# First batch's attention: gates in two passes on VectorE, products and decode kept in PSUM, q's factors from TensorE

## The chip, the cores and the metric

The kernel runs on one NeuronCore of a Trainium2 chip. The metric is the device time of one execution in microseconds (us), the median of several. The engines are TensorE (PE, with its weight loads PEld), VectorE (DVE), ScalarE (ACT) and GpSimd (POOL); SyncE (SP) issues the DMAs. Each runs its own instructions in order, and waits for the others by semaphores.

## The reference, cut to what matters

There are 4 batches of 8 heads, 768 positions and 40 features a head. An mLSTM attention is followed by a mixer of two two-layer perceptrons.

```python
for t in range(S):
    m_new = maximum(f[t] + m, i[t])
    f_stab, i_stab = exp(f[t] + m - m_new), exp(i[t] - m_new)
    C = f_stab * C + i_stab * outer(v[t], k[t]);  n = f_stab * n + i_stab * k[t]
    y[t] = sigmoid(o[t]) * (C @ q[t]) / maximum(abs(n @ q[t]), 1)
x = y.transpose(0, 2, 1, 3).reshape(4, 768, 320)
u = x + (maximum(x.T @ w_tok1, 0) @ w_tok2).T
out = u + maximum(u @ w_ch1, 0) @ w_ch2
```

## The kernel before, in words

The sequence is cut into 6 chunks of 128 positions; a unit is one batch and one chunk, u0 to u5 those of the first batch. Within a unit the attention is a masked product of scores and values, and a state `C` (40 x 41 a head) carries over what lies before it.

The gates give two rows for each head: `phi`, the running sum of the log decays within a chunk, and `b`. They come from a scan for the running maximum, two additions, a second scan and two subtractions (`gate_phi`, `gate_b`, lines 99 to 122), 36 partitions wide; `split` makes a bf16 remainder of them on 9 partitions. They are made in three passes, chunk 0, chunk 1 and chunks 2 to 5, the last one partly on GpSimd.

For the first batch TensorE spreads phi and b over a 128 x 128 tile for each head (`spread_split`), and ScalarE takes the exponential (`prep_exp`) into `dd`. `st_s` makes the scores `ps_sc` and `st_p` multiplies them into `dd` on VectorE. `prep_q3` scales q by `pq`, the exponential of phi on q's layout: for u1 and u2 from TensorE (`spread_q`), for u3 to u5 from a DMA that reads phi back from DRAM (`phi_d`, line 223). `prep_kw` scales k by `wcol`. `st_state` multiplies q with the old state into `po`, and kw with v into `pu`; VectorE masks `pu` (`bm_t`, a constant that a DMA brings) and adds the decayed state. `st_pv` adds the products with v to `po`. ScalarE copies `po` to `ht` (line 393), GpSimd multiplies it by the sigmoid of o (line 401), VectorE makes the divisor `den` (407 to 411) and the result `x` (421), and x is written as two fp32r parts, `xh` on ScalarE and `xl` on GpSimd.

The mixer's weights arrive as 30 pieces of 384 columns of 8 bytes each and are decoded beside the attention: two ScalarE operations a piece (559, 560), two VectorE operations (573, 577), the high part on ScalarE (588) and the low part on GpSimd (594). `dec_ops` is a generator of two pieces whose steps are placed by hand among other work.

The order on every engine is written out by hand in the main body (from line 696): an opening for u0 to u2 with 4 decoded pieces in it, a loop over c = 1 to 3 with two pieces a pass, and a closing part with 4 more. Then `a_part` multiplies w_tok1 with x of the six units (36 matmuls of 320 columns), and `a_end` writes its result `rh` (line 617). From there the mixer of the first batch runs in slots of one `gemm1` and one `gemm2`, with two more weight pieces a slot until all 30 are done, and later batches' attention is laid between the slots of the batch ahead. `warm` issues matmuls on zeros.

Of the kernel before, what the change touches and what calls it, by code (L numbers as in the profile page):

```python
# [18 lines left out]
L = 128  # L19
# [15 lines left out]
def kernel(ctx: ExitStack, tc: tile.TileContext, gates, qk, q3, kv, og,  # L35
                            wt1, wt2, wc1, wc2, ident, bmask, sel, out):
# [15 lines left out]
    def load_sig(b, i):  # L52
# [6 lines left out]
    floor_b = wp.tile([128, 1], F32, name="floor_b")  # L59
    nc.gpsimd.memset(floor_b, 2.0 ** -14 - 0.5)  # L60
# [36 lines left out]
    chunks = [x.rearrange("p (c t) -> p c t", t=L) for x in (b_t, d_t, phi)]  # L97

    def gate_phi(c0, c1, between=None):
        lo, hi = c0 * L, c1 * L  # L100
        sl = slice(lo, hi)
# [3 lines left out]
        if between:  # L105
            between()
        if lo == 0:
            v.tensor_tensor(d_t[:, 1:hi], f_t[:, 1:hi], m_t[:, 0:hi - 1], ALU.add)
            v.tensor_copy(d_t[:, 0:1], m_t[:, 0:1])
        else:  # L110
            v.tensor_tensor(d_t[:, sl], f_t[:, sl], m_t[:, lo - 1:hi - 1], ALU.add)
        nc.gpsimd.tensor_tensor(b_t[:, sl], i_t[:, sl], m_t[:, sl], ALU.subtract)
        v.tensor_tensor(d_t[:, sl], d_t[:, sl], m_t[:, sl], ALU.subtract)
        v.tensor_tensor_scan(phi[:, sl], rst2[:, sl], d_t[:, sl], 0.0, op0=ALU.mult, op1=ALU.add)

    def gate_b(c0, c1, eng=nc.vector):
# [200 lines left out]
    def st_state(u):  # L317
# [14 lines left out]
        if c < NC - 1:  # L332
# [36 lines left out]
    def st_pv(u, copy=True):  # L369
# [5 lines left out]
        po = t["po"] if c else ps_m.tile([128, H, E1], F32, tag="m", name="po")  # L375
# [8 lines left out]
        if u == (0, NC - 1):  # L384
            t["ht"] = po
        elif copy:
# [9 lines left out]
    def st_hs(u):  # L396
# [4 lines left out]
        (nc.vector if u == (0, NC - 1) else nc.gpsimd).tensor_tensor(sg, sg, ht[:, :, 0:D], ALU.mult)  # L401
# [12 lines left out]

    def x_ops(u):
# [126 lines left out]
    his, lows, wx = [], [], []  # L542
# [12 lines left out]
    def dec_abs(n):  # L555
        while nxt[1] < min(n, len(pieces)):
            raw = staged[nxt[1]]
            f = wq.tile([128, WP], F32, tag="wf", name="wf", bufs=4)
# [3 lines left out]
            ready[nxt[1]] = f  # L562
            nxt[1] += 1

    def dec_ops(more, m=2):
# [4 lines left out]
        ps = [(staged.pop(m), ready.pop(m)) + pieces[m] for m in range(n, min(n + m, len(pieces)))]  # L570
# [136 lines left out]
    load_phi(u0)
    load_phi(u1)
    load_phi(u2)
    nc.vector.tensor_copy(id_b, id_t)  # L710
    nc.gpsimd.tensor_tensor(id3, id_b[:, 0:H], id_b[:, 64:64 + H], ALU.add)
    nc.gpsimd.tensor_tensor(id3, id3, id_b[:, 96:96 + H], ALU.add)
    T[u0]["phi"] = r = [spread_late(ps_h, "h") for _ in range(2)]
    gate_phi(0, 1)
# [12 lines left out]
    gate_phi(1, 2, lambda: cols_out(t, 0, 1))
    gate_b(1, 2)
    split(1, 2)
    gate_d(1, 2)  # L730
# [31 lines left out]
    step(dg, 9)
    dec_abs(4)
    st_pv(u0, copy=False)
    load_kv(u2)
    dec_load(6)
    st_ht(u0)
    dec_hi()
    spread_split(u2)
    t = cols(2, NC)  # L770
    dg = dec_ops(0)
    step(dg, 3)
    cols_out(t, 2, NC)
    step(dg, 1)
    prep_exp(u2, 0)
    prep_exp(u2, 1)
    st_state(u1)
    step(dg, 9)
    spread_q(u2)
    load_pq(u2, q32)  # L780
    st_hs(u0)
    dec_low()
    prep_q3(u2)
    dec_hi()
    dec_abs(6)
    prep_kw(u2)
    load_phi(u3)
    load_qk(u3, 0)
# [251 lines left out]
```

## Time and profile before

| | us |
|---|---|
| median of 3 runs | 465.51 (465.49 to 466.0) |
| profiled execution | 467.8 |
| its span, first to last instruction | 466.0 |
| PE busy | 441.1 (95%) |
| DVE, ACT, POOL busy | 311.5, 187.0, 139.5 |
| mean granted clock of PE | 0.96 |

[...] Times in rows count from the start of the span. PE's busy time is modelled for matmuls that overlap, so a busy PE need not be one at its peak.

### The profile page before, as it was taken

What the parts mean: (1) busy time and instruction counts of PE and PEld (TensorE: products, weight loads), DVE (VectorE), ACT (ScalarE), POOL (GpSimd) and SP (SyncE); (2) the same over time, 40 slices, a digit from 0 to 9 for tenths busy, and PEclk for the clock granted to TensorE, in tenths of its full rate; (3) what the DMA queues carried; (4) which work ended last, traced back from release to release, by engine and by line L of the source; (5) the groups of instructions that cost most, each with busy time, mean ns of one, the idle gap of its engine ahead of it and who ended that gap; (6) DMA issues with size and microseconds to landing.
All of it is one profiled execution on the core that took longest, in us unless ns stands there. A gap on an engine that the chain in (4) does not pass through costs nothing.

```text
span 466.0 us, 9347 instructions
## 1 busy us (share of the span) xinstructions
PE 441.1 (95%) x3691; PEld 420.7 (90%) x3691; DVE 311.5 (67%) x665; ACT 187.0 (40%) x434; POOL 139.5 (30%) x165
## 2 busy tenths in 40 slices
PE   7669797899999998999999999999999999999997
PEld 3558686799999998999999999999999999999996
DVE  4987787877356747778888578879888555323222
ACT  4526537698634446334233335523431411212111
POOL 4466665146304435031343123034134210000000
PEclk9857878999999998999999999999999999999999
DMA  8745864576036783232274421323422000000000
GB/s 255 221 145 155 219 184 156 195 250 167 2 121 209 210 263 125 73 104 75 67 208 146 145 72 71 93 104 92 123 91 71 30 1 30 1 0 30 1 30 28
DMA packets 25032, 53.16 MB, mean 114 GB/s; under 512 B 2577, under 2 KB 13781, under 8 KB 24989
## 3 DMA queue, kind: packets, MB, share of 16 engines
q1 hardware_dynamic: 24797, 52.39, 36.8%
q8 instruction: 29, 0.48, 0.4%
q10 hardware_dynamic: 192, 0.18, 0.1%
q14 instruction: 14, 0.11, 0.1%
HBM read 48.51 MB, written 4.04 MB: 113 GB/s over the span
## 4 chain that ended last, share of the span: by engine, by line
PE 74%; DMA 10%; DVE 7%; ACT 5%; issue 2%; SPq 1%; POOL 0%; DVEq 0%; ACTq 0%
PE ps_h L600 26%; PE acc L600 25%; DMA pq<-phi_d 5%; PE ps_sc L268 4%; PE ps_a L600 4%; PE ps_b L600 4%; DVE wf L573 3%; PE po L358 3%; PE po L380 3%; DVE wf L577 2%; PE pu L337 2%; PE po L363 2%; DMA wst<-in_wt_dram 2%; DMA wst<-in_wc_dram 1%; DMA sig<-in_og_dram 1%
## 5 line engine op out<-in xcount | busy, mean ns | idle before, releaser
L600 PE MATMUL ps_h<-uT,c1h 128*128 128x256 f32 x720 | 140.3, 282 | 1.7 <-ACT uT L650 0.9
L600 PEld LDWEIGHTS ps_h<-uT,c1h 128*128 128x128 f32 x720 | 115.5, 188 | 2.8 <-ACT uT L650 1.2
L667 ACT ACTIVATE gh<-ps_h 128x512 fp32r<-128x512 f32 x72 | 42.9, 596 | 179.3 <-PE ps_h L600 179.3
L600 PE MATMUL ps_h<-uT,c1l 128*128 128x256 f32 x432 | 111.3, 280 | 0.0
L668 DVE SCALAR_TENSOR_TENSOR gl<-ps_h,gh 128x512 fp32r<-128x512 f32 x72 | 49.5, 688 | 85.8 <-ACT gh L667 85.5
L600 PE MATMUL acc<-c2h,gh 128*128 128x320 f32 x288 | 90.9, 323 | 0.0
L600 PE MATMUL acc<-c2l,gh 128*128 128x320 f32 x288 | 87.2, 310 | 0.0
L600 PEld LDWEIGHTS ps_h<-uT,c1l 128*128 128x128 f32 x432 | 81.3, 188 | 0.0
L600 PE MATMUL acc<-c2h,gl 128*128 128x320 f32 x288 | 66.4, 312 | 0.6 <-DVE gl L668 0.6
L600 PEld LDWEIGHTS acc<-c2h,gh 128*128 128x128 f32 x288 | 54.4, 189 | 1.3
L401 POOL TENSOR_TENSOR sig<-sig,ht 128x320 f32<-128x320 f32 x23 | 20.3, 883 | 114.8 <-DVE ht L366 103.4
L600 PEld LDWEIGHTS acc<-c2l,gh 128*128 128x128 f32 x288 | 54.6, 189 | 0.0
L600 PEld LDWEIGHTS acc<-c2h,gl 128*128 128x128 f32 x288 | 48.6, 190 | 1.3 <-DVE gl L668 1.3
L249 ACT ACTIVATE dd<-dd,bcol 128x128 f32<-128x128 f32 x144 | 45.8, 391 | 7.9 <-POOL dd L239 7.8
L433 POOL TENSOR_TENSOR xl<-x,xh 128x320 fp32r<-128x320 f32 x23 | 21.0, 914 | 48.9 <-DVE xh L429 46.8
L278 DVE TENSOR_TENSOR dd<-ps_sc,dd 128x512 f32<-128x512 f32 x48 | 31.1, 680 | 5.1 <-PE ps_sc L268 5.1
L573 DVE SCALAR_TENSOR_TENSOR wf<-wf,wst 128x384 int32<-128x384 int32 x30 | 25.5, 866 | 10.4 <-POOL q3t L235 4.9
L268 PE MATMUL ps_sc<-raw 40*128 40x128 f32 x384 | 30.5, 297 | 0.0
L380 PE MATMUL po<-kvt,dd 128*128 128x41 f32 (+1 forms) x192 | 26.1, 297 | 3.6 <-issue 1.8
L380 PEld LDWEIGHTS po<-kvt,dd 128*128 128x128 f32 x192 | 25.3, 210 | 4.4 <-issue 1.9
L268 PEld LDWEIGHTS ps_sc<-raw 40*128 40x128 f32 x384 | 25.6, 198 | 4.0 <-issue 2.4
L239 POOL TENSOR_SCALAR_AFFINE_SELECT dd<-dd 128x1024 f32<-128x1024 f32 x18 | 21.9, 1216 | 3.6 <-DMA dd<-phi_d 2.2
(129 smaller groups left out, 776.7 us busy)
## 6 DMA issues: line engine op xcount, KB each, us to landing
dd<-phi_d SPq DMA_DIRECT2D x18, 512.0 KB
wst<-in_wc_dram SPq DMA_DIRECT2D x22, 384.0 KB
kvt<-in_kv_dram SPq DMA_DIRECT2D x24, 324.0 KB
raw<-in_qk_dram SPq DMA_DIRECT2D x48, 160.0 KB
sig<-in_og_dram SPq DMA_DIRECT2D x8, 480.0 KB
out_dram<-x SPq DMA_DIRECT2D x24, 160.0 KB
q3t<-in_q_dram SPq DMA_DIRECT2D x20, 180.0 KB
pq<-phi_d SPq DMA_DIRECT2D x18, 180.0 KB
```

The lines of the kernel that those rows point to most:

```text
L239: nc.gpsimd.affine_select(dd, dd, pattern=[[0, H], [1, L]], compare_op=ALU.is_ge, fill=-1e30, base=0, channel_multiplier=-1)
L249: nc.scalar.activation(dd[:, h, :], dd[:, h, :], AF.Exp, bias=bcol[:, c, HP * b + h:HP * b + h + 1])
L268: nc.tensor.matmul(t["s"][hf][:, h, :], r[:, 1, h, :], r[:, 0, h, :], start=True, stop=True)
L278: nc.vector.tensor_tensor(dd, t["s"][hf], dd, ALU.mult)
L358: nc.tensor.matmul(po[:, h - h0, 0:j1 - j0], p[i][:, ROW[h], :], w[:, h, j0:j1], start=h == h0 and i + j0 == 0, stop=c == 0 and h == h1 - ...
L380: nc.tensor.matmul(o, t["dd"][:, ROW[h], :], x, start=c == 0 and h == 0, stop=h == H - 1)
L401: (nc.vector if u == (0, NC - 1) else nc.gpsimd).tensor_tensor(sg, sg, ht[:, :, 0:D], ALU.mult)
L433: (nc.vector if u == (0, 4) else nc.gpsimd).tensor_tensor(xl, x, f32(xh), ALU.subtract)
L573: v.scalar_tensor_tensor(fi, fi, 3, raw[:, :, 0], op0=ALU.logical_shift_left, op1=ALU.bitwise_or)
L600: nc.tensor.matmul(ps, a, m, start=(first and i == 0), stop=(last and i == n - 1))
L667: nc.scalar.activation(gh, ps, AF.Relu)
L668: nc.vector.scalar_tensor_tensor(gl, ps, 0.0, f32(gh), op0=ALU.max, op1=ALU.subtract)
```

## The change

The unit loop and all later batches keep their formulas. The first batch's part is rewritten. Constants that came by DMA (`sel`) or from VectorE (`id_b`) are made on GpSimd, and `z` is cleared by VectorE. The gates go in two passes, chunk 0 and chunks 1 to 5, all on VectorE.

```diff
-    def gate_phi(c0, c1, between=None):
+    def gates_of(c0, c1):
         v.tensor_tensor_scan(m_t[:, sl], f_t[:, sl], i_t[:, sl], ...)
-        nc.gpsimd.tensor_tensor(b_t[:, sl], i_t[:, sl], m_t[:, sl], ALU.subtract)
+        v.tensor_tensor(d_t[:, sd], f_t[:, sd], m_t[:, sm], ALU.add)
+        v.tensor_tensor(d_t[:, sd], d_t[:, sd], m_t[:, sd], ALU.subtract)
+        v.tensor_tensor_scan(phi[:, sl], rst2[:, sl], d_t[:, sl], 0.0, ...)
+        v.tensor_tensor(b_t[:, sl], i_t[:, sl], m_t[:, sl], ALU.subtract)
+        v.tensor_tensor(b_t[:, sl], b_t[:, sl], phi[:, sl], ALU.subtract)
 ...
     def spread_q(u):
-        ps = ps_m.tile([120, 3, L], F32, tag="m", name="ps_q")
+        ps = ps_h.tile([120, 3, L], F32, tag="h", name="ps_q")
-            nc.tensor.matmul(ps[:, g, :], sel_t[:, g * 120:(g + 1) * 120], phi[:, c * L:(c + 1) * L], ...)
+            nc.tensor.matmul(ps[:, g, :], sel3[:, g], top(z[:, 0, c * L:(c + 1) * L]), ...)
 ...
     def load_pq(u, q3t):
-            if u not in (u1, u2):
+            if b:
                 nc.sync.dma_start(out=pq.rearrange(...), in_=phi_d[...])
 ...
     def st_state(u):
+            cm = cn if c == 0 else puf
-                nc.vector.tensor_tensor(cn[0:p, a:z], puf[0:p, a:z], bm_t[0:p, a:z], ALU.mult)
+                nc.vector.tensor_tensor(cm[0:p, a:z], puf[0:p, a:z], bm_t[0:p, a:z], ALU.mult)
-                    nc.vector.scalar_tensor_tensor(cn[sl], Cst[b][sl], t["decay"][...], cn[sl], ...)
+                    nc.vector.scalar_tensor_tensor(cn[sl], Cst[b][sl], t["decay"][...], cm[sl], ...)
 ...
+    def x0_ops(u):
+        po, n = T[u]["po"], T[u]["bank"][:, 400:400 + H]
+        v.tensor_tensor(po[:, :, 0:D], po[:, :, 0:D], sig[...], ALU.mult)
+        yield
+        v.tensor_scalar(den, po[:, :, D], 1.0, None, op0=ALU.max)
+        v.scalar_tensor_tensor(n, po[:, :, D], -1.0, den, op0=ALU.mult, op1=ALU.max)
+        v.reciprocal(den, n)
+        yield
+        v.tensor_tensor(x.rearrange(...), po[:, :, 0:D], den.unsqueeze(2).to_broadcast(...), ALU.mult)
+        nc.scalar.activation(xh, x, AF.Copy)
+        (v if c == NC - 1 else nc.gpsimd).tensor_tensor(xl, x, f32(xh), ALU.subtract)
 ...
     def dec_abs(n):
-            f = wq.tile([128, WP], F32, tag="wf", name="wf", bufs=4)
+            if early[0]:
+                f = ps_acc.tile([128, WP], F32, tag="acc", name="pf")
+            else:
+                f = wq.tile([128, WP], F32, tag="wf", name="wf", bufs=4)
 ...
     def dec_ops(more, m=2):
-            v.scalar_tensor_tensor(fi, raw[:, :, 1], -0x80000000, fi, ...)
+            v.scalar_tensor_tensor(w.bitcast(I32), raw[:, :, 1], -0x80000000, f.bitcast(I32), ...)
 ...
+    for c in range(1, NC):
+        dg = dec_ops(0)
+        st_s(n1, mid=dg)                  # c < NC - 1, else step(dg, 9)
+        spread_q(n1); prep_q3(n1); prep_kw(n1)
+        dec_load(nxt[2] + 4)
+        st_state(u)
+        step(dg, 9)
+        st_pv(u)
+        load_kv(n2); load_q3(n2)
+        x0 = x0_ops(u); step(x0, 2)
+        spread_split(n2)
+        dec_hi(); prep_exp(n2, 0); prep_exp(n2, 1); dec_low()
+        dec_abs(nxt[2] + 2)
+        step(x0, 9)
+    early[0] = False
```

The loop now runs over c = 1 to 5 (the conditions on c are cut above); 10 pieces are decoded in it, none before it, and 2 after it, so that 12 stand decoded at `rh` where 14 did. `warm(10)` is added ahead of u1's spread. The SP queue brings, ahead of the loop: f, raw and kv of u0, sigmoid input, raw of u1, sigmoid input, two weight pieces, q of u1, the mask `bm_t`, kv of u1, two weight pieces, then u2's.

VectorE from the second gate pass on. Before, it works on chunks 2 to 5 after u0's products (dd), and the first mask (Cn) comes last:

```order
L278 TENSOR_TENSOR dd<-ps_sc,dd 128x512 x2
L133 COPY bcol<-gt 128x36
L103 SCALAR_TENSOR_TENSOR m_t<-f_t,m_t,i_t 36x512
L111 TENSOR_TENSOR d_t<-f_t,m_t 36x512
L113 TENSOR_TENSOR d_t<-d_t,m_t 36x512
L114 SCALAR_TENSOR_TENSOR z<-rst,d_t 36x512
L118 TENSOR_TENSOR z<-z 36x512
```

The same place now, chunks 1 to 5:

```order
L115 SCALAR_TENSOR_TENSOR m_t<-f_t,m_t,i_t 36x640
L118 TENSOR_TENSOR d_t<-f_t,m_t 36x640
L290 TENSOR_TENSOR dd<-ps_sc,dd 128x512 x2
L353 TENSOR_TENSOR Cn<-pu,bm_t 120x246
L353 TENSOR_TENSOR Cn<-pu,bm_t 80x82
L120 TENSOR_TENSOR d_t<-d_t,m_t 36x640
L122 SCALAR_TENSOR_TENSOR z<-rst,d_t 36x640
L124 TENSOR_TENSOR z<-i_t,m_t 36x640
L126 TENSOR_TENSOR z<-z 36x640
```

u0's mask, which reads `bm_t`, now stands in the middle of the second gate pass. Before, one pass of the loop on VectorE (dd: products; wf: decode; den, x: the result of the unit before):

```order
L278 TENSOR_TENSOR dd<-ps_sc,dd 128x512
L573 SCALAR_TENSOR_TENSOR wf<-wf,wst 128x384
L278 TENSOR_TENSOR dd<-ps_sc,dd 128x512
L573 SCALAR_TENSOR_TENSOR wf<-wf,wst 128x384
L407 TENSOR_SCALAR den<-ht 128x8
L577 SCALAR_TENSOR_TENSOR wf<-wst,wf 128x384
L409 SCALAR_TENSOR_TENSOR den<-ht,den 128x8
L577 SCALAR_TENSOR_TENSOR wf<-wst,wf 128x384
L411 RECIPROCAL den<-den 128x8
L341 TENSOR_TENSOR Cn<-pu,bm_t 120x246
L341 TENSOR_TENSOR Cn<-pu,bm_t 80x82
L345 SCALAR_TENSOR_TENSOR Cn<-Cn,decay 120x123 x2
```

Now (po, pu and pf lie in PSUM):

```order
L353 TENSOR_TENSOR pu<-pu,bm_t 120x246
L353 TENSOR_TENSOR pu<-pu,bm_t 80x82
L357 SCALAR_TENSOR_TENSOR Cn<-Cn,decay,pu 120x123 x2
L357 SCALAR_TENSOR_TENSOR Cn<-Cn,decay,pu 80x82
L608 SCALAR_TENSOR_TENSOR pf<-pf,wst 128x384
L611 SCALAR_TENSOR_TENSOR wf<-wst,pf 128x384 x2
L433 TENSOR_TENSOR po<-po,sig 128x8x40
L437 TENSOR_SCALAR den<-po 128x8
L438 SCALAR_TENSOR_TENSOR po<-po,den 128x8
L439 RECIPROCAL den<-po 128x8
L442 TENSOR_TENSOR x<-po,den 128x320
```

The state comes ahead of the second half of the decode, and the multiplication by the sigmoid stands on VectorE, in the unit's own pass. ScalarE in the loop before, where pq is made in place from what a DMA brought:

```order
L246 ACTIVATE dd<-ps_phi 128x512
L393 ACTIVATE ht<-po 128x328
L246 ACTIVATE dd<-ps_phi 128x512
L231 ACTIVATE pq<-pq 120x384
L588 ACTIVATE w2h<-wf 128x384 x2
```

Now pq reads TensorE's `ps_q`, and there is no copy of po:

```order
L446 ACTIVATE xh<-x 128x320
L243 ACTIVATE pq<-ps_q 120x384
L623 ACTIVATE w1h<-wf 128x384 x2
L258 ACTIVATE dd<-ps_phi 128x512 x2
L594 ACTIVATE pf<-wst 128x384
```

`pq` has moved ahead of the high parts of the weights and of the exponentials.

## Rows read from the trace of the kernel before

**Rows 1.** Windows: us; busy (instructions) PE, PEld, DVE, ACT, POOL; PE's clock, DMA share, GB/s.
```profile
20.00:40.70 20.70, 15.49 (x85) 12.46 (x85) 17.94 (x30) 7.35 (x16) 13.80 (x14) 0.52 0.43 133
40.70:64.30 23.60, 20.93 (x164) 18.92 (x163) 17.45 (x37) 12.77 (x29) 15.14 (x17) 0.78 0.74 211
76.30:122.00 45.70, 42.89 (x313) 40.87 (x313) 33.88 (x64) 37.27 (x77) 20.90 (x21) 0.99 0.59 181
```
**Rows 2.** Waits up to 76.3 us: in total, times, longest.
```profile
ACT pq L231 <- DMA pq<-phi_d: 9.8, 2, 5.5
```
**Rows 3.** Timeline, landmarks: u2's and u5's first product, a_part's result (start, duration).
```profile
35.77 0.69 DVE L278 TENSOR_TENSOR dd<-ps_sc,dd 128x512 f32<-128x512 f32 x1 [2.18 <-PE ps_sc L268]
62.26 0.68 DVE L278 TENSOR_TENSOR dd<-ps_sc,dd 128x512 f32<-128x512 f32 x1
76.30 0.44 ACT L617 ACTIVATE rh<-ps_a 128x320 fp32r<-128x320 f32 x1 [2.53 <-PE ps_a L600]
```
**Rows 4.** Timeline, VectorE: the gates' first scan, and two operations of 512 columns.
```profile
5.57 0.41 DVE L103 TENSOR_TENSOR_SCAN m_t<-f_t,i_t 36x128 f32<-36x128 f32 x1
14.51 1.26 DVE L103 TENSOR_TENSOR_SCAN m_t<-f_t,m_t,i_t 36x512 f32<-36x512 f32 x1
15.80 0.68 DVE L111 TENSOR_TENSOR d_t<-f_t,m_t 36x512 f32<-36x512 f32 x1
```
**Rows 5.** Window 0 to 14 us; timeline, ScalarE: the fourth weight piece's arrival.
```profile
0.00:14.00 14.00, 9.53 (x55) 4.59 (x56) 7.25 (x21) 5.75 (x7) 5.74 (x17) 1.00 0.85 256
...
19.88 0.55 ACT L559 ACTIVATE wf<-wst 128x384 f32<-128x384 f32 x1 [0.79 <-DMA wst<-in_wt_dram]
```
**Rows 6.** Timeline, TensorE at half clock: first and last matmul of a spread; scores.
```profile
35.60 0.61 PE L139 MATMUL ps_phi<-late_b,id_b 128*128 128x512 bf16 x1
37.71 0.63 PE L157 MATMUL ps_phi<-id,z 128*128 128x512 bf16 x1
57.75 2.08 PE L268 MATMUL ps_sc<-raw 40*128 40x128 f32 x16
```
**Rows 7.** Windows of 2 us: TensorE's clock comes back, and falls.
```profile
40.00:42.00 2.00, 2.00 (x19) 2.00 (x19) 0.22 (x2) 1.02 (x3) 0.45 (x1) 1.00 0.04 8
52.00:54.00 2.00, 0.31 (x3) 0.15 (x2) 0.55 (x1) 0.86 (x3) 0.22 (x2) 0.92 0.96 300
```
**Rows 8.** Timeline, VectorE: operations of the loop and of the closing part.
```profile
39.57 0.54 DVE L577 SCALAR_TENSOR_TENSOR wf<-wst,wf 128x384 int32<-128x384 int32 x1
42.31 0.56 DVE L341 TENSOR_TENSOR Cn<-pu,bm_t 120x246 f32<-120x246 f32 x2 [2.09 <-PE pu L337]
50.27 0.50 DVE L341 TENSOR_TENSOR Cn<-pu,bm_t 120x246 f32<-120x246 f32 x2
50.73 0.82 DVE L345 SCALAR_TENSOR_TENSOR Cn<-Cn,decay 120x123 f32<-120x123 f32 x3
58.18 0.83 DVE L407 TENSOR_SCALAR den<-ht 128x8 f32<-128x8 f32 x1
60.67 0.50 DVE L341 TENSOR_TENSOR Cn<-pu,bm_t 120x246 f32<-120x246 f32 x2
69.29 0.49 DVE L421 TENSOR_TENSOR x<-sig,den 128x320 f32<-128x320 f32 x1
69.70 0.48 DVE L401 TENSOR_TENSOR sig<-sig,po 128x320 f32<-128x320 f32 x1
70.10 0.16 DVE L407 TENSOR_SCALAR den<-ht 128x8 f32<-128x8 f32 x1
```
**Rows 9.** Timeline, VectorE: two slots with decode; chain: a slot's two products without decode.
```profile
105.05 0.68 DVE L668 SCALAR_TENSOR_TENSOR gl<-ps_h,gh 128x512 fp32r<-128x512 f32 x1
109.17 0.68 DVE L668 SCALAR_TENSOR_TENSOR gl<-ps_h,gh 128x512 fp32r<-128x512 f32 x1
...
124.00 1.89 PE ps_h L600 x16
125.88 1.76 PE acc L600 x12
```

More of the change, by code (lines that the diff above doesn't have):

```diff
@@ L134, in cols_out, with cols_w, cols_w_out @@
+        yield
+    def cols_w(c0, c1):
+        n = c1 - c0
+        t = ps_m.tile([128, n, B * HP], F32, tag="m", name="gw")
+        e = id_t[0:B * HP, 0:B * HP]
+        for i in range(n):
+            a, z = (c0 + i) * L, (c0 + i + 1) * L
+            nc.tensor.matmul(t[:, i], b_t[:, a:z], e, start=True, stop=False)
+            nc.tensor.matmul(t[:, i], phi[:, z - 1:z].to_broadcast([B * HP, 128]), e, start=False, stop=True)
+        return t
+    def cols_w_out(t, c0, c1):
         nc.scalar.activation(wcol[:, c0:c1, :].rearrange("p c (b g i) -> p (c b) i g", b=B, g=3),
-                             t[:, 1].rearrange("p c (b i g) -> p (c b) i g", b=B, g=3), AF.Exp)
+                             t.rearrange("p c (b i g) -> p (c b) i g", b=B, g=3), AF.Exp)
@@ L137, in spread_late, with cols_b @@
+    def cols_b():
+        t = ps_m.tile([128, NC, B * HP], F32, tag="m", name="gt")
+        for c in range(NC):
+            nc.tensor.transpose(t[:, c], b_t[:, c * L:(c + 1) * L], id_t[0:B * HP, 0:B * HP])
+        nc.vector.tensor_copy(bcol, t)
     def spread_late(pool, tag):
@@ L383, in st_pv @@
         t["po"] = po
[L384 to L386 removed]
+        if b:
             st_ht(u)
@@ L391, in st_ht @@
         po = t["po"]
-        ht = (ep if u[0] == 0 and u[1] % 2 else ap).tile([128, H, E1], F32, tag="ht", name="ht", bufs=1)
+        ht = ap.tile([128, H, E1], F32, tag="ht", name="ht", bufs=1)
         nc.scalar.activation(ht, po, AF.Copy)
@@ L569, in dec_ops @@
         v = nc.vector
-        ps = [(staged.pop(m), ready.pop(m)) + pieces[m] for m in range(n, min(n + m, len(pieces)))]
+        ps = [(staged.pop(m),) + ready.pop(m) + pieces[m] for m in range(n, min(n + m, len(pieces)))]
         for raw, f, *_ in ps:
@@ L709 @@
[L709 to L714, printed above, removed]
+    for u in us[0:3]:
+        load_phi(u)
+    load_sig(0, 0)
     load_qk(u1, 0)
     load_qk(u1, 1)
+    load_sig(0, 1)
     dec_load(2)
-    q31 = load_q3t(u1)
+    q3s = {u1: load_q3t(u1)}
     nc.sync.dma_start(out=bm_t, in_=bmask)
-    gate_b(0, 1)
+    load_kv(u1)
@@ L721 @@
+    dec_load(4)
+    load_qk(u2, 0)
+    load_qk(u2, 1)
+    q3s[u2] = load_q3t(u2)
+    load_kv(u2)
+    T[u0]["phi"] = r = [spread_late(ps_h, "h") for _ in range(2)]
+    g = gates_of(0, 1)
+    step(g, 9)
     split(0, 1)
-    gate_d(0, 1)
     spread_phi(r, 0)
-    t = cols(0, 1)
-    T[u1]["phi"] = r1 = [spread_late(ps_acc, "acc") for _ in range(2)]
+    t = cols_w(0, 1)
     st_s(u0, mult=False)
[L727 to L730, printed above, removed]
@@ L753 @@
-    st_s(u1, mult=False)
+    sigmoid(0)
+    g = gates_of(1, NC)
+    step(g, 2)
+    st_p(u0)
+    st_state(u0)
+    st_pv(u0)
+    st_s(u1, mult=False)
+    step(g, 9)
+    split(1, 2)
+    dec_abs(2)
+    warm(10)
+    spread_split(u1)
+    t = cols_w(1, NC - 1)
+    spread_q(u1)
     prep_exp(u1, 0)
     prep_exp(u1, 1)
-    load_pq(u1, q31)
-    gate_d(2, NC, nc.gpsimd)
+    load_pq(u1, q3s[u1])
     prep_q3(u1)
+    cols_w_out(t, 1, NC - 1)
     prep_kw(u1)
-    st_p(u1, dg)
-    st_state(u0)
@@ L762 @@
[L762 to L768, printed above, removed]
-    spread_split(u2)
[L770 to L774, printed above, removed]
+    split(2, 3)
+    spread_split(u2)
+    x0 = x0_ops(u0)
+    step(x0, 2)
+    st_p(u1)
+    step(x0, 9)
     prep_exp(u2, 0)
     prep_exp(u2, 1)
[L777 to L788, printed above, removed]
-    load_qk(u3, 1)
-    dec_load(8)
-    load_q3(u3)
+    load_pq(u2, q3s[u2])
+    split(3, NC)
     gp.release()
@@ L794 @@
     xpool[2] = ep
-    dec_low()
-    for c in range(1, NC - 2):
+    load_phi(us[3])
+    load_qk(us[3], 0)
+    load_qk(us[3], 1)
+    for c in range(1, NC):
         u, n1, n2, n3 = (units[c + i] for i in range(4))
         dg = dec_ops(0)
-        st_s(n1, mid=dg)
+        if c < NC - 1:
+            st_s(n1, mid=dg)
+        else:
+            step(dg, 9)
         if c < 3:
             load_phi(n3)
-        load_kv(n2)
-        if c < 3:
             load_qk(n3, 0)
             load_qk(n3, 1)
-        den = st_den(units[c - 1])
-        for _ in dg:
-            next(den, None)
+        if c < NC - 1:
+            spread_q(n1)
+            prep_q3(n1)
+            prep_kw(n1)
@@ L810 @@
         dec_load(nxt[2] + 4)
+        st_state(u)
+        if c == NC - 1:
+            for i in range(1, NC - 2):
+                a_part(0, 0, i)
+                a_part(0, 1, i)
+        step(dg, 9)
+        st_pv(u)
+        if c < 4:
+            load_kv(n2)
+            load_q3(n2)
+        x0 = x0_ops(u)
+        step(x0, 2)
+        if c == 2:
+            nc.sync.dma_start(out=phi_d.rearrange("c r t -> r c t"), in_=phi.rearrange("p (c t) -> p c t", t=L))
+        if c < 4:
+            spread_split(n2)
@@ L846 @@
-    dec_load(nxt[2] + 4)
-    dec_hi()
-    dec_low()
-    dec_abs(nxt[2] + 2)
-    st_pv(u5)
-    st_hs(u5)
-    den = [st_den(u4), st_den(u5)]
-    for _ in range(3):
-        for d in den:
-            step(d)
-    den = [x_ops(u4), x_ops(u5)]
-    for _ in range(3):
-        for d in den:
-            step(d)
+            cols_b()
+        if c == 4:
+            load_sig(1, 1)
+    early[0] = False
     dg = dec_ops(0)
     step(dg, 5)
-    for i in range(1, NC - 1):
+    for i in range(NC - 2, NC - 1):
```

205 lines of the change are left out of this document (81 added, 124 removed).

## The prediction

> **What bounds the kernel now.** Start with the page: 441.1 of 466.0 us of span are TensorE's, at a mean clock of 0.96. Such an average hides stages with other limits, so cut the span by landmarks and read each stretch by windows. From 76.3 to 122 TensorE works 42.89 of 45.7 us at 0.99 [rows 1]: the mixer is bound by its products, and apart from one more decode slot the change moves nothing there. Before the landmark the stretch from 20 to 40.7 has clock 0.52, and 40.7 to 64.3 has 0.78 [rows 1]; neither is full of products. So what is to be won lies before `rh` at 76.30, and 1 us earlier there is 1 us off the whole.
>
> Inside that stretch the landmarks are u2's first product on VectorE at 35.77, u5's at 62.26 and `rh` at 76.30 [rows 3]: an opening, three passes in 26.5 us, and a closing part of 14.0. The waits say why passes are long: ScalarE stood 9.8 us in two waits for pq read back from DRAM, 5.5 in one [rows 2]. [...] The distance between u2's, u3's and u4's first masks shows both kinds of pass: 42.31 to 50.27 is 7.96 with the clock up, 50.27 to 60.67 is 10.40 with a pq wait and half the clock [rows 8]. VectorE's own operations also stretch: `den`'s first took 0.83 at 58.18 and 0.16 at 70.10 [rows 8], the same 128x8 tile.
>
> **Opening.** The cast that stood ahead of the first scan (at 5.57, [rows 4]) goes; I start the gates at 4.9, between 3.4 if only f's arrival counts and 5.5 if nothing is saved. The first pass took about 2.8 and ends at 7.7. The second now covers 640 columns: from 1.26 and 0.68 for 512 [rows 4], a scan is 1.57 and an addition 0.85. With u0's two products (0.68 each) the sum is 7.7 + 1.57 + 0.85 + 1.36 = 11.5.
>
> Then comes a new wait. u0's mask stands in the middle of that gate pass, and needs `bm_t`, which SP sends behind two weight pieces. Adding the tiles on the queues up to it gives 3.4 MB, at 256 GB/s [rows 5] 13.3 us. Calibrate that: the fourth weight piece of before had 4.58 MB up to its end, 17.9 us by the same rate, and ScalarE waited for it until 19.88 [rows 5], 2.0 more. So the mask starts at about 15.3 (13.3 if that lag is the tail's alone), after 3.8 us of idle VectorE. Queued behind it: the rest of the gates, one scan (1.57) and three additions (2.55), and the split, priced as a fourth (0.85). With the mask pair at 0.50 [rows 8] they end at 15.3 + 0.5 + 1.57 + 2.55 + 0.85 = 20.8. All of TensorE's next work waits for that; `warm(10)` cannot cover it, since it needs the PSUM slot which the same mask frees. I therefore expect half clock again. A spread is then 2.74 [rows 6], so u1's ends at 23.5. Small transposes and q's factors, estimated at 1.6 (eight and three matmuls; the twelve of that spread are 0.23 apart, the smallest need less; bounds 0.8 to 2), and u2's spread bring 27.8, exponential and first product 29.0. With the clock up all of this halves, and with the mask at 13.3, u2 starts near 26; with scores (2.08 at half clock, [rows 6]) and another late transfer in the chain, 32. Taken: 29.0, which is 6.8 before 35.77.
>
> **A pass of the loop.** pq now comes from TensorE, so both DMA waits go; next to be late is VectorE. Its own list in a pass: two products at 0.68, four decode steps at 0.54, mask pair 0.50, state 0.82, sigmoid product 0.48, three small ones about 0.5 in all, result 0.48 or 0.49 [rows 3, 8]: 6.3 us. TensorE's spread, scores, pv and state at full clock are shorter and run beside it. Bounds: 6.3 if VectorE never waits, 7.96 if nothing is saved against the open pass of before. What no row shows is VectorE or ScalarE writing PSUM, as `pu`, `po` and `pf` now make them do. Reading it is free within the rows: 128x320 took 0.48 with a PSUM operand and 0.49 without [rows 8]. Far bounds for a write are thus that −0.01, and +0.67, `den`'s worst against its best [rows 8]. The nearest row, the one with `po`, is near the lower end, so I take 0.1 for each of eight such steps. That and the hand-over from TensorE to ScalarE's exponentials make 7.2 a pass. GpSimd's product and ScalarE's copy of po go; the former is the 0.48 counted in VectorE's list, the latter is worth nothing here, as ScalarE was busy 12.77 of the 23.6 us of the loop [rows 1]. Three passes: 21.6 against 26.5, 4.9 saved; u5's product at 50.6.
>
> [...]
>
> **Closing and decode.** From u5's product to `rh` I keep 14.0 [rows 3]: fewer waits on pq stand against two more decoded pieces (12 at its end, 14 before, but four of before's were in the opening). Bounds 12.5 and 18, the last if TensorE is at half clock. So `rh` is at 64.6, 11.7 earlier. The two pieces that are missing make one more mixer slot with decode: such slots are 4.12 apart [rows 9], a slot without is 1.89 + 1.76 = 3.65, so +0.5; below it nothing if the piece hides elsewhere, above it 2 if a piece comes late, since decoding now leads use by two slots where it led by three.
>
> **Sum.** −6.8 − 4.9 + 0 + 0.5 = −11.2. The profiled execution took 467.8 (span 466.0 and 1.8 around it), 2.3 above the median 465.51; that offset is its own, so I subtract from both: 456.6 for a profiled one, 454.3 for the median.
>
> **Rivals.**
> Dearer pass: a PSUM write costs 0.3 on eight steps, or the transfers of a pass (raw, kv, q and two pieces, 1.6 MB, 6.4 us at 256 GB/s, [rows 5]) come late, and a pass is 9. For it: 300 GB/s at full DMA share stood where TensorE idled [rows 7]. Against: two pieces a pass went through the 7.96 pass too. Time: 3 × 1.8 = 5.4 more, 459.7.
>
> No stall: `bm_t` is there in time or the clock holds through the opening, u2 at 26 and passes of 6.3: 3 + 2.7 less, 448.6. For it: 1.00 was held for 14 us at the start [rows 5]. Against: the queue's order.
>
> Slower: the stall's idle time takes the clock, and since VectorE paces the loop TensorE is too sparse to get it back. Then the pass is before's cold one, 10.4 [rows 8], and the closing part 18. u5 at 29.0 + 31.2 = 60.2, `rh` at 78.2, with the slot +2.4: 467.9. It decides from a pass of about 9.5 in a cold loop (11.0 where the closing part stays at 14.0). For it: 0.52 held for the 20 us from 20 on, and a VectorE-paced pass loads TensorE less. Against: before came back at 40 to 42 with such passes [rows 7], and it fell only at a DMA wait that is gone.
>
> That the change does not do what it says, hardly: pq's read-back is not issued for the first batch.
>
> **Chances.** Forecast 0.60 (its own range 451 to 458), dearer pass 0.20, no stall 0.12, slower 0.08. A difference within 0.2% (0.93 us) can't be told from no change by this measurement. The slower case lies mostly beyond it, and the edge between it and the dearer pass gives the middle: faster 0.90, same 0.03, slower 0.07. The range takes both sides' ends: 448.3 with no stall, and 29 raised to 32, a pass of 7.96 and a late piece (3 + 2.3 + 1.5) above, 461.
>
> **What would show it.** VectorE idle for 3 to 4 us ahead of u0's mask, ended by `bm_t`; no wait of ScalarE on pq's DMA in the first batch; u2's product at 29, u5's at 50.6, 7.2 between masks; `den`'s first at 0.16 in the loop; the clock near 0.5 from 18 to 29 and up from the loop on; `rh` at 64.6; one more slot of 4.1. I am wrong in the opening if u2's product is not between 26 and 32, in the loop if masks are over 8 apart, and in the whole if time goes back after `rh`.

## The result, and the profile after

The changed kernel takes 452.21 us (median of 4, 450.38 to 453.32) against 465.5 (464.37 to 466.0) of before: ratio 0.9714, 95% interval 0.9677 to 0.9751. Its profiled execution took 453.3 with a span of 451.5, so 14.5 less than the 467.8 and 466.0 of before. A kernel's ratio leaves out runs more than 1.5% above its fastest (mask_early, gp_product, mask_early_warm_close and mask_early_sig_warm below have one each), and its median does not.

The landmarks of the changed kernel, from its timeline (start, duration, engine, line; in brackets the idle time before and what ended it), with u0's mask, which waited, ahead of them and one pass of the loop between them:

```profile
17.46 0.56 DVE L353 TENSOR_TENSOR Cn<-pu,bm_t 120x246 f32<-120x246 f32 x2 [5.40 <-DMA bm_t<-in_bmask_dram]
...
29.20 0.69 DVE L290 TENSOR_TENSOR dd<-ps_sc,dd 128x512 f32<-128x512 f32 x1
...
35.38 0.68 DVE L290 TENSOR_TENSOR dd<-ps_sc,dd 128x512 f32<-128x512 f32 x1
36.43 0.57 DVE L608 SCALAR_TENSOR_TENSOR pf<-pf,wst 128x384 int32<-128x384 int32 x1 [0.37 <-ACT wst L595]
36.90 0.68 DVE L290 TENSOR_TENSOR dd<-ps_sc,dd 128x512 f32<-128x512 f32 x1
37.50 0.69 DVE L353 TENSOR_TENSOR pu<-pu,bm_t 120x246 f32<-120x246 f32 x2
38.32 0.80 DVE L357 SCALAR_TENSOR_TENSOR Cn<-Cn,decay,pu 120x123 f32<-120x123 f32 x3
39.04 0.56 DVE L608 SCALAR_TENSOR_TENSOR pf<-pf,wst 128x384 int32<-128x384 int32 x1
39.50 1.01 DVE L611 SCALAR_TENSOR_TENSOR wf<-wst,pf 128x384 int32<-128x384 int32 x2
40.43 0.49 DVE L433 TENSOR_TENSOR po<-po,sig 128x320 f32<-128x320 f32 x1
40.95 0.17 DVE L437 TENSOR_SCALAR den<-po 128x8 f32<-128x8 f32 x1
...
41.60 0.49 DVE L442 TENSOR_TENSOR x<-po,den 128x320 f32<-128x320 f32 x1
42.01 0.68 DVE L290 TENSOR_TENSOR dd<-ps_sc,dd 128x512 f32<-128x512 f32 x1
...
48.91 0.68 DVE L290 TENSOR_TENSOR dd<-ps_sc,dd 128x512 f32<-128x512 f32 x1
...
61.68 0.82 ACT L652 ACTIVATE rh<-ps_a 128x320 fp32r<-128x320 f32 x2 [1.08 <-issue]
```

Against [rows 3], u2's first product is 6.57 us earlier, the three passes take 19.71 instead of 26.49 (6.78 less), and from u5's product to `rh` it is 12.77 instead of 14.04 (1.27 less): 14.62 in all. Read the pass from 35.38 to 42.01 as a list: one operation follows another, with 0.37 us of idle time that has a releaser. VectorE's list is the pass, 6.63 us.

The windows of the opening and the loop (columns as in [rows 1]; PE's clock is the granted share of its full speed):

```profile
15.00:18.00 3.00, 0.00 (x0) 0.00 (x0) 0.54 (x3) 2.71 (x5) 0.00 (x0) 1.00 0.87 269
18.00:22.00 4.00, 3.70 (x10) 1.46 (x12) 3.90 (x6) 0.25 (x1) 0.00 (x0) 0.57 0.77 270
22.00:26.00 4.00, 3.52 (x31) 2.69 (x30) 3.77 (x11) 1.20 (x2) 0.00 (x0) 1.00 0.35 133
26.00:49.00 23.00, 21.43 (x218) 18.28 (x219) 21.31 (x53) 14.10 (x32) 16.40 (x21) 1.00 0.55 166
```

TensorE does nothing for 3 us, runs at about half clock (0.57) from 18 to 22, and is back at full clock before the spreads; the loop then keeps 1.00, where [rows 1] showed 0.52 and 0.78. And the waits (in total, times, longest): the first two of the opening, the last of the stretch from 150 to 166 us, in the second batch:

```profile
DVE Cn L353 <- DMA bm_t<-in_bmask_dram: 5.4, 1, 5.4
...
PE warm L729 <- DVE Cn L353: 3.3, 1, 3.3
...
ACT pq L243 <- DMA pq<-phi_d: 4.3, 1, 4.3
```

The 9.8 us of [rows 2] are gone from the first batch. After `rh` the profiled execution gains nothing more: the ninth decode slot costs 0.62 (`gl` is VectorE's operation of a slot; from the first to the one at 122.04 it is 49.05, before 48.43), and 0.5 comes back in what else stands behind `rh`.

### The profile page after: what moved, and what is told of

Same layout as the page of the kernel before. It is cut to its first block, busy times and chain, and to the rows that moved or that the text cites. A ratio compares the mean times of both kernels' runs of the same rounds, so it can differ in the third digit from the quotient of the medians.

```text
span 451.5 us, 9377 instructions
## 1 busy us (share of the span) xinstructions
PE 434.0 (96%) x3717; PEld 413.8 (92%) x3718; DVE 304.9 (68%) x664; ACT 187.0 (41%) x429; POOL 126.1 (28%) x159
## 4 chain that ended last, share of the span: by engine, by line
PE 77%; DVE 4%; ACT 2%; DMA 1%; issue 1%; POOL 1%; DVEq 0%; ACTq 0%; SPq 0%
PE ps_h L635 27%; PE acc L635 26%; PE ps_sc L280 4%; PE ps_a L635 4%; PE ps_b L635 4%; PE po L370 3%; PE po L396 2%; DVE wf L608 2%; PE pu L348 2%; PE po L375 2%; DMA wst<-in_wc_dram 1%; DVE wf L611 1%; PE po L340 1%; ACT wf L594 1%; ACT wst L595 1%
## 5 line engine op out<-in xcount | busy, mean ns | idle before, releaser
L415 POOL TENSOR_TENSOR sig<-sig,ht 128x320 f32<-128x320 f32 x18 | 14.8, 824 | 112.6 <-DVE ht L378 102.3
L465 POOL TENSOR_TENSOR xl<-x,xh 128x320 fp32r<-128x320 f32 x18 | 15.8, 877 | 47.2 <-DVE xh L463 47.2
L280 PE MATMUL ps_sc<-raw 40*128 40x128 f32 x384 | 28.6, 285 | 0.0
L280 PEld LDWEIGHTS ps_sc<-raw 40*128 40x128 f32 x384 | 23.9, 187 | 3.7 <-issue 1.7
L396 PE MATMUL po<-kvt,dd 128*128 128x41 f32 (+1 forms) x192 | 23.6, 280 | 1.7 <-issue 1.7
L396 PEld LDWEIGHTS po<-kvt,dd 128*128 128x128 f32 x192 | 22.8, 194 | 1.9 <-issue 1.9
L251 POOL TENSOR_SCALAR_AFFINE_SELECT dd<-dd 128x1024 f32<-128x1024 f32 x18 | 22.9, 1273 | 3.7 <-DMA dd<-phi_d 1.9
L303 DVE TENSOR_TENSOR r<-dd 128x512 f32<-128x512 f32 x24 | 22.6, 979 | 0.0
```

What stands on the lines that cost most here:

```text
L251: nc.gpsimd.affine_select(dd, dd, pattern=[[0, H], [1, L]], compare_op=ALU.is_ge, fill=-1e30, base=0, channel_multiplier=-1)
L280: nc.tensor.matmul(t["s"][hf][:, h, :], r[:, 1, h, :], r[:, 0, h, :], start=True, stop=True)
L303: nc.vector.tensor_tensor(r[:, h], dd[:, h], top(dd)[:, h], ALU.subtract)
L396: nc.tensor.matmul(o, t["dd"][:, ROW[h], :], x, start=c == 0 and h == 0, stop=h == H - 1)
L415: nc.gpsimd.tensor_tensor(sg, sg, ht[:, :, 0:D], ALU.mult)
L465: nc.gpsimd.tensor_tensor(xl, x, f32(xh), ALU.subtract)
```

## The experiments

All medians stand against 452.2 of the changed kernel; the kernel before, at 465.5 beside the changed one, took 464.8 to 465.7 beside the experiments. "To `rl`" is VectorE's first operation on `rh`, at 62.90 in the changed kernel, 33.70 after u2's product.

**mask_early.** u0's mask is sent sooner.

```diff
     load_kv(u0)
+    nc.sync.dma_start(out=bm_t, in_=bmask)
...
     q3s = {u1: load_q3t(u1)}
-    nc.sync.dma_start(out=bm_t, in_=bmask)
```

> bm_t is sent right behind u0's kv instead of behind two weight pieces. In the changed kernel VectorE stood 5.40 us for it, and u2's first product was at 29.20. Theory A: that wait lies whole on VectorE's chain to u2's product. Then the mask follows u0's products at about 12.1, u2's product is at 24 to 25, rh's second half at about 57 and the time 447 to 448. Rival B: what u1 needs next (its kv and q, u2's raw, all behind weight pieces, or TensorE) takes the wait's place. Then u2's product is at 27.5 or later and the time 450.5 to 452.

Measured: 448.13 (ratio to before 0.9622, 0.956 to 0.9683, which just touches the changed kernel's 0.9677 to 0.9751). Its timeline:

```profile
12.03 0.55 DVE L353 TENSOR_TENSOR Cn<-pu,bm_t 120x246 f32<-120x246 f32 x2
...
23.77 0.69 DVE L290 TENSOR_TENSOR dd<-ps_sc,dd 128x512 f32<-128x512 f32 x1
```

Both are 5.43 us earlier, the whole wait of 5.40: theory A. The wait that the change brought in was on the path, through VectorE.

**no_warm** and **mask_early_no_warm** leave out the line `warm(10)`, with bm_t late and early.

> warm(10) ahead of u1's spread is left out; bm_t stays late. Theory A: TensorE is at half clock for u1's spread, transposes and u2's spread, and VectorE covers part of it: u2's product at about 30.5, time 453 to 454. Rival B: VectorE paces the opening alone: u2's product stays at 29.2 and the time at 452.2. Rival C: the clock, once low, does not come back in a loop paced by VectorE: passes of 9 to 10 us instead of 6.6, time 460 or more.

> bm_t early and no warm(10). With bm_t early TensorE has u1's scores up to about 15 and waits for the split until about 18.7. Theory A: that gap costs the clock, the spreads take 2.74 and not 2.0, and the time is 1 to 2 us above that of bm_t early alone. Rival B: no difference, since VectorE paces the opening.

Measured: 457.08 and 449.51. no_warm by windows:

```profile
18.00:24.00 6.00, 1.88 (x11) 1.15 (x10) 5.66 (x12) 0.60 (x1) 0.00 (x0) 0.50 0.71 244
24.00:32.00 8.00, 8.00 (x46) 6.24 (x47) 3.70 (x6) 2.82 (x6) 2.64 (x4) 0.54 0.04 15
32.00:52.00 20.00, 18.60 (x192) 16.24 (x188) 18.02 (x49) 11.92 (x26) 12.54 (x17) 1.00 0.63 191
```

TensorE does the spreads at half clock, and VectorE waits for it: u2's product comes at 32.40 (28.30 with bm_t early), 3.2 and 4.5 later. Theory A, larger than I put it for no_warm; B falls. C falls too: the clock comes back in the loop, whose passes stay at 6.18, 6.62 and 6.90. Where the cost goes later, mask_early_no_warm tells: 4.5 us late at u2 and 5.9 late at `rl` (63.34 against 57.47), its median is only 1.4 above mask_early's; the place that gives it back comes at the end of this section.

**pq_dma** brings pq of u3 to u5 from DRAM again.

```diff
-            if b:
+            if b or c > 2:
                 nc.sync.dma_start(out=pq.rearrange(...), in_=phi_d[...])
...
+            if n1[1] < 3:
                 spread_q(n1)
```

The store of phi moves from the pass of c = 2 to the end of the gates.

> For u3, u4 and u5 pq is read back from DRAM again, as before the change; phi is stored to DRAM as soon as the gates are done. All else as changed. Theory A: the read-back was what made the passes long. Then ScalarE waits for it again, 2 us or more in each of two or three passes, TensorE's clock falls, and the time is 456 to 462. Rival B: with the rest of the change the transfer lands in time, and the time stays within 451 to 453; then the gain of the loop came from VectorE's list and not from pq.

Measured: 457.37 (454.8 to 459.13). Its waits from 30 to 62, and a window:

```profile
ACT pq L243 <- DMA pq<-phi_d: 7.2, 3, 3.2
```

```profile
46.00:52.00 6.00, 4.23 (x35) 4.04 (x32) 4.65 (x13) 4.63 (x10) 4.02 (x6) 0.77 0.97 294
```

Theory A: the transfer is late again, 7.2 us in three waits at a DMA share of 0.97; TensorE's work thins out and the clock falls to 0.77. From u2's product to `rl` it is 37.18, 3.5 more. But only 0.65 of that lies in the three passes (6.18, 6.62 and 7.56), and the rest behind u5's product. So rival B has a part in it: with the other parts of the change in place, the read-back alone does not bring the old passes of 8.8 us back.

**gp_product** takes the result by the old way.

```diff
-        v.tensor_tensor(po[:, :, 0:D], po[:, :, 0:D], sig[...], ALU.mult)
+        st_ht(u)
+        st_hs(u)
+        po, ht = T[u]["fin"]
         yield
-        v.tensor_scalar(den, po[:, :, D], 1.0, None, op0=ALU.max)
+        v.tensor_scalar(den, ht[:, :, D], 1.0, None, op0=ALU.max)
```

> The first batch's result goes by the old way again: ScalarE copies po out of PSUM, GpSimd multiplies by the sigmoid, VectorE makes the divisor and x from the copies; the rest as changed. In the changed kernel a pass of the loop is 6.6 us and VectorE is idle 0.4 of it. Theory A: what moved to VectorE pays by sparing a hand-over (ScalarE 0.43, GpSimd 0.8 and its stretching of VectorE's operations) that VectorE would wait for in its own order: passes of 7.5 or more, time 455 to 457. Rival B: VectorE's list alone sets a pass; without the product of 0.48 it is shorter: passes of 6.2, time 450 to 451.

Measured: 457.71 (455.61 to 463.09), u2's product at 33.12, passes of 9.01, 7.45 and 6.30. In the opening VectorE stood 4.1 us for ScalarE's copy, which is the second of these lines (the third is VectorE's wait):

```profile
26.39 0.49 ACT L243 ACTIVATE pq<-ps_q 120x384 f32<-120x384 f32 x1 [1.62 <-PE ps_q L182]
...
26.96 0.45 ACT L407 ACTIVATE ht<-po 128x328 f32<-128x328 f32 x1
...
27.44 0.66 DVE L437 TENSOR_SCALAR den<-ht 128x8 f32<-128x8 f32 x1 [4.07 <-ACT ht L407]
```

The copy stands behind pq, which waits for TensorE. So the time goes as theory A has it, but 3.9 of the 8.4 us up to `rl` by the place that the copy got in ScalarE's order, and more by the clock that was lost there (0.74 from 30 to 50, 0.58 in the first pass). In the second pass the clock is 1.00, and there the stretching of theory A shows: beside GpSimd, `den`'s first two steps and `x` take 0.77, 0.92 and 0.94 with their operands in SBUF, against 0.17, 0.17 and 0.49 in the changed kernel. The third pass, 6.30, is what B expected. So the old path is dearer in some passes and not in others.

**decode_sbuf** sets `early = [False]`, so that `pf` lies in SBUF.

> The decode's intermediates of the first batch lie in SBUF again and not in PSUM. Theory A (a PSUM operand costs nothing, an SBUF pair is stretched by GpSimd): VectorE's four decode operations, 0.5 each in the changed kernel, take up to 0.8 beside GpSimd's work, a pass is 0.5 to 1 longer, time 454 to 457. Rival B (PSUM spared nothing): they stay at 0.5, time 452.

Measured: 457.11 (454.11 to 459.01). Timelines of VectorE and of GpSimd in one pass:

```profile
36.27 0.56 DVE L608 SCALAR_TENSOR_TENSOR wf<-wf,wst 128x384 int32<-128x384 int32 x1 [0.37 <-ACT wst L595]
...
38.88 1.14 DVE L608 SCALAR_TENSOR_TENSOR wf<-wf,wst 128x384 int32<-128x384 int32 x1
39.95 1.54 DVE L611 SCALAR_TENSOR_TENSOR wf<-wst,wf 128x384 int32<-128x384 int32 x2
...
38.60 1.00 POOL L247 TENSOR_TENSOR q3t<-q3t,pq 120x384 f32<-120x384 f32 x1
39.56 1.04 POOL L270 TENSOR_TENSOR kw<-kvt,wcol 128x320 f32<-128x320 f32 x1
```

Theory A. The same operation takes 0.56 with GpSimd idle and 1.14 beside its `q3t`; in the changed kernel it is 0.56 beside the same `q3t` (38.76 to 39.77). Three passes take 22.63, 2.9 more, and from u2's product to `rl` it is 39.74, 6.0 more.

**state_sbuf** sets `cm = cn`.

> The masked pu goes to SBUF (Cn) again, and the decayed state is added to it there; later batches are changed likewise. In the changed kernel the mask pair writes PSUM in 0.69; before, it wrote SBUF in 0.50. Theory A: the write into PSUM costs 0.19 a pair; without it a pass is 0.2 shorter, four passes 0.8, time 451.4. Rival B: the sum in SBUF reads two SBUF operands and is stretched by GpSimd (over 0.80), and nothing is won or up to 1 us is lost: 452 to 453.

Measured: 455.62 (453.62 to 457.37). VectorE and GpSimd:

```profile
37.24 0.55 DVE L353 TENSOR_TENSOR Cn<-pu,bm_t 120x246 f32<-120x246 f32 x2
37.76 2.00 DVE L357 SCALAR_TENSOR_TENSOR Cn<-Cn,decay 120x123 f32<-120x123 f32 x3
...
38.55 1.11 POOL L247 TENSOR_TENSOR q3t<-q3t,pq 120x384 f32<-120x384 f32 x1
```

Both theories name a true effect, and B decides, larger than expected: the mask is 0.14 cheaper into SBUF, and the sum of two SBUF operands takes 2.00 instead of 0.80. u2's product to `rl` is 3.6 us longer.

**mask_early_split** and **three_passes** change the gates, with bm_t early: `split(3, NC, nc.gpsimd)` right behind the gates instead of VectorE's, and chunk 1 apart from chunks 2 to 5.

```diff
     step(g, 9)
+    split(3, NC, nc.gpsimd)
     split(1, 2)
...
-    split(3, NC)
```

```diff
-    g = gates_of(1, NC)
-    step(g, 2)
+    step(gates_of(1, 2), 9)
+    split(1, 2)
+    g = gates_of(2, NC)
     st_p(u0)
```

> bm_t early, and the bf16 remainders of chunks 3 to 5 (0.95 and 1.78 on VectorE, right ahead of u2's product) are made on GpSimd, as soon as the gates are done; GpSimd stood idle there. Theory A: VectorE's list paces the opening, so u2's product comes 2 to 2.7 earlier than with bm_t early alone (21 to 22 instead of 23.77), time 445.5 to 446.5. Rival B: u2's scores on TensorE (from 22.16) or ScalarE's exponentials take the place: 0.5 to 1 won. Rival C: GpSimd's split, beside VectorE's SBUF work, stretches it by as much as it takes away: nothing won, 448.

> bm_t early, and the gates in three passes on VectorE (chunk 0, chunk 1, chunks 2 to 5) as before the change, instead of two. Theory A: VectorE paces the opening, and the third pass adds six short operations (0.3 to 0.4 each) less some 0.3 an operation saved by 512 columns for 640: about 1 us more, u2's product at 24.8 instead of 23.77, time 449. Rival B: u1's spread starts sooner (at about 11), TensorE and ScalarE are ahead, and the time is the same or up to 1 us less.

Measured: 447.75 (445.04 to 449.09) and 449.47 (447.77 to 450.96), u2's product at 25.97 and 26.63 where mask_early has 23.77. The splits on VectorE beside GpSimd's in the first, and u1's and u2's products in the second:

```profile
16.79 1.57 DVE L161 TENSOR_TENSOR z<-z 9x256 f32<-9x256 f32 x1
18.40 1.57 DVE L160 TENSOR_TENSOR z<-z 9x256 f32<-9x256 f32 x1
```

```profile
21.84 1.35 DVE L290 TENSOR_TENSOR dd<-ps_sc,dd 128x512 f32<-128x512 f32 x2 [1.79 <-ACT dd L258]
...
26.63 0.69 DVE L290 TENSOR_TENSOR dd<-ps_sc,dd 128x512 f32<-128x512 f32 x1 [1.09 <-PE ps_sc L280]
```

The first is rival C and more: two operations of the splits, 0.42 each, take 1.57 beside GpSimd's, and the spread behind them starts late. In the second VectorE waits 1.79 for ScalarE, which waits for a spread that stands behind scores and `warm`'s products at a lower clock (0.76 from 10 to 24; 1.00 in mask_early). Three passes cost 2.9 us at u2 in this profile, more than A's 1, and a good part by TensorE's clock and not by the count of operations. How much belongs to the passes is open: in mask_early_sig, whose opening is mask_early's, the clock also fell (0.88 from 10 to 24), and u2's product came at 24.78. In neither did the median follow by as much.

**mask_early_sig, mask_early_warm_close, mask_early_sig_warm** look for the place that takes or gives back some 4 us in the second batch. The edits are `c in (1, 3)` for `c in (3, 4)` in the loading of the next batch's sigmoid inputs, and a line `warm(7)` ahead of the end of a_part.

> bm_t early, and in the later batches the next batch's sigmoid inputs (480 KB each) are loaded two and one units sooner, so that they no longer stand ahead of the last two units' pq. With bm_t early alone, ScalarE stood 3.1 us for pq's read-back in the second batch (until 152.68), TensorE was short of work for 0.94 of 156 to 158 and ran at half clock until about 165. Theory A: the same read-back that the change removed from the first batch still costs the second one about 4 us. Then pq lands about 2 us sooner, the clock stays up there, and the time is 444 to 446, with less spread from run to run. Rival B: what holds TensorE there is the mask and the exponentials behind phi's 512 KB, and nothing is won: 448.

> bm_t early, and seven products on zeros on TensorE ahead of the last part of w_tok1 times x, where TensorE waited 1.4 us for xh and then ran at half clock for some 4 us (0.62 from 61.7 to 65 in the changed kernel). Theory A: the wait takes the clock; filled, the first products of the mixer run at full clock and 1 to 2 us are won: 446 to 447. Rival B: the mixer's start waits for ScalarE and VectorE there, and nothing is won.

> All three: bm_t early, sigmoid inputs earlier, seven products on zeros ahead of the closing. If the terms are independent, the gains add: 442.5 to 445.

Measured: 447.96, 447.15 and 448.73; none is distinct from mask_early's 448.13. The earlier sigmoid inputs only moved the wait: in mask_early_sig TensorE's clock fell from 142 on (0.50 from 146 to 150) instead of from 158, and in mask_early_sig_warm it fell behind 160 again (0.66 from 160 to 165). The filled gap at the closing won nothing, as the profile of mask_early has the full clock there without it (`rl` at 57.44 and 57.47). But these runs show what the place does. Windows of mask_early, and of mask_early_warm_close, whose profiled execution took 444.6, in the same stretch:

```profile
155.00:160.00 5.00, 3.99 (x27) 3.81 (x26) 2.61 (x5) 2.12 (x6) 1.91 (x2) 0.82 0.27 103
160.00:165.00 5.00, 5.00 (x21) 5.00 (x20) 4.46 (x9) 4.54 (x8) 3.42 (x4) 0.50 0.51 157
```

```profile
155.00:160.00 5.00, 4.89 (x39) 4.71 (x38) 3.06 (x7) 3.28 (x10) 2.73 (x3) 1.00 0.46 133
160.00:165.00 5.00, 5.00 (x42) 4.81 (x42) 4.21 (x7) 3.27 (x4) 2.98 (x3) 1.00 0.40 139
```

The gap of about 1 us takes the clock for some 7 (0.55 from 158 to 160, 0.50 to 164, 0.75 to 166), and from `rl` to the end it is 389.4 us in the one and 385.4 in the other, with the same code there. What differs ahead of the gap is the landing of the last pq, on ScalarE in the one and in the other:

```profile
152.68 0.52 ACT L243 ACTIVATE pq<-pq 120x384 f32<-120x384 f32 x1 [3.11 <-DMA pq<-phi_d]
```

```profile
151.72 0.53 ACT L243 ACTIVATE pq<-pq 120x384 f32<-120x384 f32 x1 [2.67 <-DMA pq<-phi_d]
```

It is 0.96 us later in mask_early, and TensorE's gap ahead of its next products on `po` is 1.01 us there against 0.11. Why the same transfer lands at two times no run tells. mask_early_no_warm keeps the full clock in this place, and it too takes 385.4 from `rl` on: that is where most of its lateness is given back. Runs without a profile go the same way by their mean clock: mask_early_sig took 445.4 at a clock of 1.000 and 451.2 at 0.981.

## Why the prediction was right, and which terms were off

The total: −11.2 was forecast, −13.3 came between the medians and −14.5 between the profiled executions, inside the range, by the mechanisms that it names. Step by step:

**The opening's size was right for the wrong reasons.** 6.8 earlier was forecast, 6.57 came. The step "the mask starts at about 15.3" failed by 2.2 us: it started at 17.46, as bm_t came 4.2 us behind its bytes at 256 GB/s, where 2.0 was taken from another transfer. The step "`warm(10)` cannot cover it ... I therefore expect half clock" failed in the other direction: half clock was there from 18 to 22 only (0.57), and it was `warm(10)`, released by that same mask, that ran through it and gave the spreads the full clock. no_warm shows the half clock that I had forecast (0.50 to 0.54 from 18 to 32), and with it u2's product comes at 32.40 and not at 29.0. The third step that failed is the path: from the mask to u2's product I counted 13.7 us of TensorE's cold chain, and what paces that stretch is VectorE's list, 11.74 us almost without a gap:

```profile
17.46:29.20 11.74, 10.42 (x73) 6.53 (x75) 11.31 (x19) 4.08 (x9) 2.34 (x3) 0.85 0.42 150
```

Behind the gates it holds 7.4 us (the splits, u0's result, u1's products), of which I had priced one split at 0.85. So mask_early gains the whole wait. 2.2 us too early and 2.0 us too long cancel, which is luck.

**The pass: 7.2 forecast, 6.57 on average measured.** The mechanism (pq's waits go, VectorE's list is next) was right for the changed kernel: no wait on pq is left, and pq_dma brings back 7.2 us of waits and 3.5 us of time. That those waits alone made the passes long is not borne out, as only 0.65 of the 3.5 lies in the passes. The mis-sized term is 0.1 for each of eight steps that write PSUM. Only the mask pair got dearer, 0.69 for 0.55 in state_sbuf; `pf`, `po` and the state are within 0.03 of their list prices. The rivals of a dearer pass (9) and of a cold loop (10.4) are excluded by passes of 6.18, 6.63 and 6.90 at clock 1.00. (The range's lower end, 448.3, should be the 448.6 of the case that it names.)

**What I had not priced is what PSUM spares.** The prediction read `den`'s 0.83 against 0.16 [rows 8] as a bound for an unknown write. GpSimd was at work beside the first (the first line here) and not beside the second, and that is the price to look at.

```profile
57.80 1.18 POOL L433 TENSOR_TENSOR xl<-x,xh 128x320 fp32r<-128x320 f32 x1
58.95 1.19 POOL L401 TENSOR_TENSOR sig<-sig,ht 128x320 f32<-128x320 f32 x1
...
58.93 0.54 DVE L577 SCALAR_TENSOR_TENSOR wf<-wst,wf 128x384 int32<-128x384 int32 x1
```

With the intermediates in SBUF the state takes 2.00 for 0.80 and the decode 1.14 for 0.56 beside GpSimd, and such a stretch is on the path where VectorE's list is the pass. With one operand in PSUM the decode step takes 0.56 beside the same work of GpSimd (`q3t`, 38.76 to 39.77), and the state's 0.80 runs beside it too (38.32 to 39.12); without the 0.8 that I added for the writes the sum was 6.4. That is not the whole of it, though. `den`'s 0.83 is an operation with one SBUF input, and an SBUF pair is not stretched each time: right behind that `den` a decode step with two SBUF inputs kept its 0.54, while GpSimd's product beside it took 1.19 (0.81 in gp_product). What decides when a pair is stretched no run shows.

As a source, PSUM was no dearer than SBUF in these traces: from `po` in PSUM L433 and L442 took 0.48 to 0.50 and L437 0.17, where [rows 8] have 0.49 (L421) and 0.16 (L407) from SBUF.

**Closing and slot.** 14.0 was kept, 12.77 came; what shortened it no run tells apart, though pq has a part in it: pq_dma lost 2.8 of its 3.5 us there. The added slot cost 0.62 for 0.5.

**Not settled.** The four parts undone alone (pq, result, decode, state) lose 5.2, 5.5, 4.9 and 3.4 us by their medians, more together than the 13.3 of the change. So they do not add; that each holds only while the others keep VectorE's list short and TensorE's clock up is my reading, and no run undoes two of them together. The opening's 6.57 is not divided up either: gates in two passes against three were tried only with bm_t early.

The best kernels are those with bm_t early: 448.13 us, and 447.15 to 447.96 with further edits that can't be told from it.

## What to carry to other kernels

Where one engine's list is a pass, look at each of its operations for a second operand in the memory that a neighbour reads too: moving one operand elsewhere (4.9 and 3.4 us here) can be worth about as much as moving the operation (5.5). Where a change puts a new consumer of a transfer into an in-order engine's list, follow that transfer's place in its queue first; here one line gave 4 us. And a gap of 1 us on the engine with the clock can cost 4, as in the second batch here.

## What the runs showed of the hardware

That last point I had not expected: the second batch still reads pq back from DRAM, and its last wait (4.3 us of ScalarE in the changed kernel) leaves TensorE short of work. In the changed kernel:

```profile
162.00:164.00 2.00, 0.66 (x5) 0.63 (x5) 1.97 (x5) 0.00 (x0) 1.28 (x2) 1.00 0.21 83
164.00:166.00 2.00, 2.00 (x13) 2.00 (x14) 0.44 (x1) 1.34 (x5) 0.63 (x1) 0.72 0.16 57
166.00:168.00 2.00, 2.00 (x9) 2.00 (x9) 1.46 (x4) 1.98 (x6) 0.81 (x1) 0.50 0.52 154
```

The kernel before has the same dip, from 176 on:

```profile
176.00:178.00 2.00, 0.40 (x4) 0.43 (x4) 1.92 (x4) 0.18 (x1) 1.02 (x2) 1.00 0.19 78
...
180.00:182.00 2.00, 2.00 (x10) 2.00 (x9) 1.27 (x4) 1.98 (x7) 0.81 (x1) 0.50 0.65 165
```

Of the profiled executions, the six that keep the full clock in this place take 385.4 to 387.3 us from `rl` to the end, and the seven of the changed kernel and its variants that do not, 387.4 to 390.6. Runs of one kernel differ by up to 6 us, most likely by this for the greater part, and comparisons of less than 2 us between medians decide nothing here.
